# Class-ordered tokens, separate transpose banks and 72-query dilated tiles in a fused attention and MLP kernel

## Chip, core and metric

The kernel runs on one core of one Trainium2 chip. Its engines are TensorE (PE; its weight loads are listed apart as PEld), VectorE (DVE), ScalarE (ACT), GpSimd (POOL) and SyncE (SP, which here only issues transfers). The metric is the device time of that core in microseconds (us), lower is better. Three timed runs of the kernel before gave 463.66, 466.44 and 466.76 us; the median is 466.44 us.

## What is computed

Eight batches, eight heads, 576 tokens, head size 64. Heads 0 to 3 attend to the last 32 tokens; heads 4 to 7 to 32 tokens in steps of 4 (the same residue modulo 4). The result, 4608 tokens by 512, goes through a two-layer MLP with a swish-like gate.

```python
rel = pos[:, None] - pos[None, :]
mask_plain = (rel >= 0) & (rel < 32)
mask_dil = (rel >= 0) & (rel < 32 * 4) & (rel % 4 == 0)
attn = softmax(where(mask, q @ k.T / 8, -1e9))       # heads 0-3 plain, 4-7 dilated
x = (attn @ v).transpose(0, 2, 1, 3).reshape(8 * 576, 512)
h = x @ w_in                                         # 512 -> 2048
out = (h / (1 + exp(-beta * h))) @ w_out             # 2048 -> 512, float32
```

## The kernel before, in words

Every engine executes its instructions in program order, and the order is written out by hand. Attention of one batch is a list of 44 named steps (`STEPS`). The MLP works on nine tiles of 512 tokens (t = 0 to 8); tile t is 16 `slot_h` (four matmuls of 512 columns into a bank of `psum_h`, two banks; then a tanh on ACT and a `g` on DVE) and 16 `slot_o` (four matmuls each; four slots complete one block of 128 tokens in the only bank of `psum_o`, then ACT copies it to `osb` and SP stores it). Attention of batch 0 runs alone; after that the loop over t issues the slots of tile t with the steps of batch t + 1 between them, about one and a half steps a slot. Eight `slot_o` of a tile follow its last `slot_h`, the other eight are mixed into the next tile. Tiles 7 and 8 have no attention beside them, and the last tile ends with 16 `slot_o`.

Heads are handled in pairs x = 0 to 3 (x = 0, 1 plain, called h = 0; x = 2, 3 dilated, h = 1). Steps:

- T (`step_t`, two for each x): a row of the loaded q or k holds four consecutive tokens, T = 0 to 3 being the residue modulo 4. Six transposes of 96 rows (L192) fill one bank `tp` with k and q of two residues. DVE then copies k to `kT` (L201), ACT half of q to `qz` (L202), DVE the other half (L203). For h = 0 the copies write with a step of four elements, because `kT` and `qz` are in token order; for h = 1 they are in class order (residue after residue), and the copies write runs.
- S (`step_s`): two matmuls give the scores of two query tiles of 96 against 128 keys (L210), ACT takes the exponential into `pt` (L216), DVE multiplies by a mask (L220).
- V (`step_v`): four matmuls (L230) into the only bank of `psum_pv`; DVE takes the reciprocal of the sums (L236) and scales (L238) into `xs`.
- X (`step_x`): two transposes (L252) into a `tp` bank, and one to four ACT copies (L271) into `xT`, split where a tile of 512 tokens or a residue ends. For h = 1 these write with a step of four.

The two `tp` banks are shared by T and X. `extras(b)` says beside which step POOL casts the next batch (`cast_qk`, `cast_v`) and SP loads the one after (`load_qk`, `load_v`, `fill_v`). The dilated v is loaded by 12 transfers in rows of 256 bytes. `first` does the same for batch 0 and for the weights, which POOL issues. `tick` issues a store two slots after its block.

Of the kernel before, what the change touches and what calls it, by code (L numbers as in the profile page):

```python
# [23 lines left out]
def kernel(  # L24
# [17 lines left out]
    WIN = 32  # L42
    QT = 96
# [36 lines left out]
    kT = [const_pool.tile([P, WIN + S], BF16, name=f"kT{i}") for i in range(4)]  # L80
    qz = [const_pool.tile([P, 2, S], BF16, name=f"qz{i}") for i in range(4)]
    pt = [const_pool.tile([P, NI * 2 * QT + WIN], BF16, name=f"pt{i}") for i in range(4)]
    vaug = [[const_pool.tile([P, NI, 4, D + 1], BF16, name=f"vaug{p}{h}") for h in range(2)]
            for p in range(2)]
    vst = [vstage_pool.tile([P, NI, 4, D], FP32, name=f"vst{h}") for h in range(2)]
    xT = {}


    def zeros():
        for i in range(4):  # L90
            nc.vector.memset(qz[i][64:128, 0, :], 0.0)
            nc.vector.memset(qz[i][0:64, 1, :], 0.0)
            nc.vector.memset(kT[i][:, 0:WIN], 0.0)
            nc.vector.memset(pt[i][:, NI * 2 * QT:], 0.0)
        for p in range(2):
            for h in range(2):
                nc.vector.memset(vaug[p][h][:, :, :, D:D + 1], 1.0)
        for h in range(2):
            nc.vector.memset(vst[h][0:WIN, :, :, :], 0.0)

    def build_masks():
        pp = masks["PP"]
        flat = pp[:].rearrange("p a b n -> p (a b) n")
        nc.gpsimd.memset(flat, 1.0)

        nc.gpsimd.affine_select(
            out=flat, in_=flat, pattern=[[0, 4], [-1, QT]], base=-1, channel_multiplier=1,
            compare_op=ALU.is_ge, fill=0.0)
        nc.gpsimd.affine_select(
            out=flat, in_=flat, pattern=[[0, 4], [1, QT]], base=WIN, channel_multiplier=-1,  # L110
            compare_op=ALU.is_ge, fill=0.0)
        for name, m in masks.items():
            if name == "PP":
                continue
            nc.vector.tensor_copy(out=m[:], in_=pp[:])
            for a in range(2):
                if name[a] == "F":
                    nc.vector.memset(m[0:WIN, a, :, :], 0.0)
                if name[a] == "M":
                    nc.vector.memset(m[0:80, a, :, 48:QT], 0.0)  # L120

    def build_beta():
        tpb = psum_pv.tile([P, 4, P], FP32, name="pv")
        nc.tensor.transpose(tpb[:, 0, 0:NFB], beta_row[:, :], ident_f[:, :])
        nc.vector.tensor_single_scalar(
            out=beta_half[:], in_=tpb[:, 0, 0:NFB], scalar=0.5, op=ALU.mult)
# [300 lines left out]
```

## Time and profile before

| what | value |
|---|---|
| median of three runs | 466.44 us |
| the profiled execution | 463.03 us, span of its instructions 461.3 us |
| PE busy | 356.1 us (77% of the span), 2305 matmuls and transposes |
| PEld busy | 180.7 us (39%) |
| DVE busy | 263.7 us (57%) |
| ACT busy | 228.8 us (50%) |
| POOL busy | 81.1 us (18%) |
| mean granted TensorE clock | 0.925 of 2.4 GHz |

Busy times are shares of the whole span. The span has stages with different limits: attention of batch 0 alone, seven tiles with attention beside the MLP, two tiles of MLP alone. Matmuls are pipelined, so the time from the start of one to the start of the next says more than the length of one.

### The profile page before, as it was taken

To read this page: it belongs to the slowest core of one execution; us is meant where nothing else is said; L and a number is where in the kernel's file an instruction comes from. 1 tells how busy PE (TensorE), PEld (TensorE's weight loads), DVE (VectorE), ACT (ScalarE), POOL (GpSimd) and SP (SyncE) were. 2 spreads that over 40 slices of the span, in tenths; PEclk is the share of its full clock that TensorE was granted. 3 is DMA by queue.
4 is the path that set the end of the run, shared out by engine and by line. 5 is a ranking of instruction groups with operands and counts; after the bars stand their busy time and mean duration, and the time that the engine had idled before them with its cause. 6 is when DMAs were issued, how large, how long until landed. Compare 5 with 4: busy or idle time off the path is not lost.

```text
span 461.3 us, 6491 instructions
## 1 busy us (share of the span) xinstructions
PE 356.1 (77%) x2305; PEld 180.7 (39%) x2305; DVE 263.7 (57%) x604; ACT 228.8 (50%) x515; POOL 81.1 (18%) x119
## 2 busy tenths in 40 slices
PE   1156577859886978867985798697886899999986
PEld 0133343424443434434442454343443444444432
DVE  7676568456853667267736765466726682532510
ACT  1245366536554456435743565345643665544521
POOL 2243445025000520044003400052000000000000
PEclk9999999977998789959997989878995999999999
DMA  8989987930555015710862055500020001001011
GB/s 204 203 166 214 195 194 186 240 87 1 134 133 147 1 52 133 181 50 1 185 163 68 0 140 129 148 1 31 0 77 0 11 14 60 33 24 45 23 47 69
DMA packets 68609, 43.72 MB, mean 95 GB/s; under 512 B 40912, under 2 KB 63456, under 8 KB 68576
## 3 DMA queue, kind: packets, MB, share of 16 engines
q1 hardware_dynamic: 61920, 37.62, 32.3%
q0 software_dynamic: 4224, 4.19, 5.5%
q10 hardware_dynamic: 2432, 1.48, 1.4%
q8 instruction: 18, 0.29, 0.3%
q14 instruction: 15, 0.12, 0.1%
HBM read 36.71 MB, written 9.44 MB: 100 GB/s over the span
## 4 chain that ended last, share of the span: by engine, by line
PE 38%; DVE 10%; ACT 7%; issue 1%; POOL 0%; ACTq 0%
PE o_ps L302 19%; PE h_ps L286 15%; DVE g L293 3%; ACT tnh L290 3%; DVE kT L201 2%; ACT osb L307 2%; ACT qz L202 2%; DVE qz L203 2%; DVE pt L220 1%; PE pv L230 1%; PE sc L210 1%; DVE xs L238 1%; PE tp L192 1%; PE tp L252 1%; ACT pt L216 0%
## 5 line engine op out<-in xcount | busy, mean ns | idle before, releaser
L286 PE MATMUL h_ps<-xT,w_in_bf 128*128 128x512 bf16 x576 | 159.8, 408 | 0.8 <-DVE g L293 0.7
L293 DVE SCALAR_TENSOR_TENSOR g<-tnh,h_ps 128x512 bf16<-128x512 bf16 x144 | 98.9, 687 | 104.2 <-ACT tnh L290 102.9
L302 PE MATMUL o_ps<-w_out_bf,g 128*128 128x512 bf16 x576 | 149.7, 395 | 9.8 <-ACT osb L307 9.8
L290 ACT ACTIVATE tnh<-h_ps,beta_half 128x512 bf16<-128x512 f32 x144 | 98.6, 685 | 51.5 <-PE h_ps L286 51.5
L176 POOL CAST qkb<-stage 96x512 bf16<-96x512 f32 x84 | 49.5, 627 | 199.4 <-PE tp L192 162.3
L202 ACT COPY qz<-tp 64x288 bf16<-64x288 bf16 x64 | 37.8, 591 | 88.2 <-DVE kT L201 88.2
L302 PEld LDWEIGHTS <-g 128*128 128x128 bf16 x576 | 54.6, 101 | 62.3 <-issue 18.3
L192 PE MATMUL tp<-ident_b,qkb 96*128 96x96 bf16 x384 | 34.0, 242 | 58.2 <-DVE qz L203 38.7
L286 PEld LDWEIGHTS <-w_in_bf 128*128 128x128 bf16 x576 | 55.3, 104 | 50.6 <-issue 11.6
L203 DVE COPY qz<-tp 64x288 bf16<-64x288 bf16 x64 | 35.5, 555 | 42.4 <-ACT qz L202 42.4
L192 PEld LDWEIGHTS <-qkb 96*128 96x128 bf16 x384 | 28.6, 117 | 74.0 <-issue 44.6
L271 ACT COPY xT<-tp 128x96 bf16<-128x96 bf16 (+4 forms) x174 | 42.3, 355 | 18.9 <-PE tp L252 18.9
L230 PE MATMUL pv<-vaug,pt 128*128 128x65 bf16 x384 | 30.1, 203 | 26.6 <-DVE xs L238 25.9
L307 ACT ACTIVATE osb<-o_ps 128x512 f32<-128x512 f32 x36 | 21.5, 597 | 54.9 <-PE o_ps L302 54.9
L216 ACT ACTIVATE pt<-sc 128x384 bf16<-128x384 f32 x96 | 45.5, 482 | 6.1 <-PE sc L210 6.1
L230 PEld LDWEIGHTS <-pt 128*128 128x128 bf16 x384 | 21.7, 103 | 55.1 <-DVE xs L238 44.1
L238 DVE TENSOR_TENSOR xs<-pv,rcp 96x256 bf16<-96x256 f32 x96 | 40.3, 420 | 3.3
L210 PE MATMUL sc<-qz,kT 128*128 128x192 bf16 x192 | 35.2, 274 | 5.4 <-ACT pt L216 5.3
L201 DVE COPY kT<-tp 128x288 bf16<-128x288 bf16 x64 | 35.1, 549 | 1.1 <-PE tp L192 0.3
L210 PEld LDWEIGHTS <-kT 128*128 128x128 bf16 x192 | 19.6, 109 | 27.0 <-issue 15.1
L179 POOL CAST vaug<-vst 128x1536 bf16<-128x1536 f32 x16 | 23.8, 1490 | 33.2 <-DMA vst<-in_v_dram 24.2
L236 DVE RECIPROCAL rcp<-pv 96x4 f32<-96x4 f32 x96 | 16.7, 174 | 21.3 <-PE pv L230 21.2
(40 smaller groups left out, 102.4 us busy)
## 6 DMA issues: line engine op xcount, KB each, us to landing
out_dram<-osb SPq DMA_DIRECT2D x36, 256.0 KB, 2.0
stage<-in_k_dram SPq DMA_DIRECT2D x16, 384.0 KB, 4.7
stage<-in_q_dram SPq DMA_DIRECT2D x14, 384.0 KB, 5.8
vst<-in_v_dram SPq DMA_DIRECT2D x96, 48.0 KB, 3.8
vst<-in_v_dram SPq DMA_DIRECT2D x30, 144.0 KB, 5.9
stage<-in_q_dram SPq DMA_DIRECT2D x16, 192.0 KB, 4.9
stage<-in_k_dram SPq DMA_DIRECT2D x14, 192.0 KB, 4.6
w_in_bf<-in_moe_w_in_dram POOLq DMA_DIRECT2D x4, 512.0 KB, 7.4
```

Source lines behind the costliest of these rows:

```text
L176: (eng.copy if eng is nc.scalar else eng.tensor_copy)(out=o[:, hp], in_=i[:, hp])
L192: nc.tensor.transpose(tp[:, j, c * QT:(c + 1) * QT], src[:, c, hp, 2 * tt + j].rearrange("p a d -> p (a d)"), ident_b[0:QT, 0:QT])
L202: nc.scalar.copy(out=view(qd[0:64, 0, :]), in_=tp[0:64, :, 144:288])
L203: nc.vector.tensor_copy(out=view(qd[64:128, 1, :]), in_=tp[64:128, :, 144:288])
L210: nc.tensor.matmul(sc[:, a, 0:2 * QT], lhsT=kT[x][:, i * QT:i * QT + P], rhs=qz[x][:, :, i * QT:(i + 1) * QT], start=True, stop=True)
L216: nc.scalar.activation(out=w.rearrange("p (a n) -> p a n", a=2), in_=sc[:, :, 0:2 * QT], func=ACT.Exp, scale=SCALE)
L230: nc.tensor.matmul(pv[:, h4, 0:D + 1], lhsT=pt[2 * h + hp][:, c:c + P], rhs=vaug[b % 2][h][:, i, h4, :], start=True, stop=True)
L238: nc.vector.tensor_tensor(out=xs[:], in0=pv[0:QT, :, 0:D], in1=rcp[0:QT, :].unsqueeze(2).to_broadcast([QT, 4, D]), op=ALU.mult)
L286: nc.tensor.matmul(hps[:], lhsT=w_in_bf[:, kt, fb * P:(fb + 1) * P], rhs=xT[t][:, kt, :], start=(kt == 0), stop=(kt == NKT - 1))
L290: nc.scalar.activation(out=tnh[:], in_=hps[:], func=ACT.Tanh, scale=beta_half[:, fb:fb + 1])
L293: nc.vector.scalar_tensor_tensor(out=g[:], in0=tnh[:], scalar=1.0, in1=hps[:], op0=ALU.add, op1=ALU.mult)
L302: nc.tensor.matmul(ops[:], lhsT=g_t[t, fb][:, tb * P:(tb + 1) * P], rhs=w_out_bf[:, fb, :], start=(fb == 0), stop=(fb == NFB - 1))
```

## The change

All tokens stay in class order (residue after residue in each batch) from the load to the output rows. Part by part:

- T is split in K (`step_k`) and Q (`step_q`), four each, with eight transposes in a bank of their own. K has one DVE copy of 576 columns, for x = 0, 1 reading the bank with a step and writing runs. Q has two copies of 576 columns by one engine: DVE for x = 1, else ACT.
- Dilated queries are cut into tiles of 72 (one class is 144): for x = 2, 3 four S steps of 2 x 144 columns and four V steps of two tiles; for x = 0, 1 three S steps and two V steps of three tiles. A V step now works on one pair of heads.
- X: three or four transposes in one bank and one ACT copy of 288 columns, eight a batch. `xT` is one tensor for all 4608 tokens.
- Dilated v comes in two transfers with rows of 1 KB.
- Blocks of 128 rows are stored by class, one transfer for each class that they touch. `osb` has two buffers instead of three, and in the last tile every other block uses a bank of `psum_h`.
- Order: 42 steps; `at_once` lets 3, 2, then 1 block of a tile (4 in the last) follow its last `slot_h`, the rest is mixed into the next tile. Steps are paced by weights (`WORK`), with twice as many beside a `slot_o` as beside a `slot_h`. Loads of dilated v, weights and the next batches are issued beside other steps.

```diff
 STEPS = (
-    "T00 T01 T02 T03 T10 S000 T11 S010 T12 S001 T13 S011 S002 V00 S012 V01 S100 V02 X00 "
-    "S110 V03 X01 S101 V04 X02 S111 V05 X03 S102 V10 X04 S112 V11 X05 V12 X10 V13 X11 V14 "
-    "X12 V15 X13 X14 X15"
+    "K0 Q0 K1 Q1 S00 K2 S01 Q2 S02 K3 S10 Q3 S11 V00 S12 V01 S20 X00 S21 V10 S22 X01 V11 S23 "
+    "X10 S30 V20 X11 S31 V21 S32 V22 X20 S33 V23 V30 X21 V31 V32 X30 V33 X31"
 ).split()
...
-    osb_pool = pool("osb", 3)
+    osb_pool = pool("osb", 2)
...
-    xT = {}
+    xT = const([P, NKT, B * S], BF16, "xT")
...
+        else:
+            rows = v[b, 4:8].rearrange("h (t T) d -> t h (T d)", T=C)
+            e(0).dma_start(out=vd_st[0:96, 0].rearrange("p h T d -> p h (T d)"), in_=rows[0:96])
+            e(1).dma_start(out=vd_st[:, 1].rearrange("p h T d -> p h (T d)"), in_=rows[16:CT])
...
+    def transposes(b, x, chunks, lo):
+        h, hp = divmod(x, 2)
         src = qkb[b, h]
+        tp = psum_tp.tile([P, 1024], BF16, name="tp")
+        tv = tp[:, 0:8 * QT].rearrange("p (T t) -> p T t", T=C)
+        for T in range(C):
+            for i, c in enumerate(chunks):
                 nc.tensor.transpose(
+                    tv[:, T, i * QT:(i + 1) * QT],
+                    src[:, c, hp, T].rearrange("p a d -> p (a d)"), ident_b[0:QT, 0:QT])
+        return tv[:, :, lo:lo + CT]
+
+    def step_k(b, x):
+        tv = transposes(b, x, (0, 1), 0)
+        if x < 2:
+            nc.vector.tensor_copy(
+                out=kT[x][:, WIN:].rearrange("p (t T) -> p t T", T=C),
+                in_=tv.rearrange("p T t -> p t T"))
         else:
+            nc.vector.tensor_copy(out=kT[x][:].rearrange("p (T t) -> p T t", T=C), in_=tv)
+
+    def step_q(b, x):
+        tv = transposes(b, x, (1, 2), 48)
+        copy = nc.vector.tensor_copy if x == 1 else nc.scalar.copy
+        copy(out=qz[x][0:64, 0], in_=tv[0:64])
+        copy(out=qz[x][64:128, 1], in_=tv[64:128])
...
+    def step_v(b, x, j):
+        h, hp = divmod(x, 2)
+        n, m = (QT, 3) if x < 2 else (HT, 2)
+        pv = psum_pv.tile([P, 512], FP32, name="pv")
...
+            nc.scalar.copy(
+                out=o.rearrange("p T (i u) -> p T i u", i=3),
+                in_=xp[:, 0:m * n].rearrange("p (i T u) -> p T i u", i=3, T=C))
         else:
+            nc.scalar.copy(out=o, in_=xp[:, 0:m * n].rearrange("p (T t) -> p T t", T=C))
...
         if part == 0:
-            o_t[t, tb] = psum_o.tile([P, HD], FP32, name="o_ps")
+            if t == NTT - 1 and tb % 2:
+                o_t[t, tb] = psum_h.tile([P, HD], FP32, name="h_ps")
+            else:
+                o_t[t, tb] = psum_o.tile([P, HD], FP32, name="o_ps")
...
+               lambda: load_w_in(1), lambda: load_w_in(2), lambda: load_w_in(3),
+               lambda: load_qk(1, 0, [SQ]), lambda: load_v(1, 0, [SQ])],
+        "S00": [build_beta],
+        "S20": [lambda: load_w_out(0), lambda: load_w_out(1)],
+        "S22": [lambda: load_w_out(2), lambda: load_w_out(3),
+                lambda: load_qk(1, 1, [SQ]), lambda: load_v(1, 1, [SQ])],
...
+    at_once = [3, 2] + [1] * (NTT - 3) + [4]
+    WORK = {"K": 3, "Q": 4, "S": 3, "V": 3, "X": 2}
...
+        room = [(1 if fn is slot_h else 2) for fn, *_ in slots[:-2]]
+        total, whole, done, seen = sum(room), sum(WORK[s[0]] for s in STEPS), 0, 0
```

For t = 3 to 6 this gives the order (h and o are slots): h K0 h Q0 o K1 Q1 h o S00 K2 h S01 o Q2 S02 h K3 h S10 o Q3 h S11 o V00 S12 h V01 o S20 X00 h S21 h V10 o S22 X01 h V11 o S23 X10 h S30 o V20 X11 h S31 h V21 o S32 V22 h X20 o S33 V23 h V30 o X21 V31 o V32 X30 o V33 X31 o o. The tiles have 28, 28, 28, 32, 32, 32, 32, 32 and 44 slots, before 24, then 32 seven times, then 40.

## Rows read from the trace of the kernel before

**Rows 1.** Stretches: PE, PEld, DVE, ACT, POOL busy us (count); PE clock, DMA share, GB/s.

```profile
9.50:45.50 36.00, 16.41 (x145) 10.90 (x146) 25.47 (x64) 15.82 (x41) 12.73 (x16) 1.00 1.05 194
45.50:92.50 47.00, 34.84 (x243) 17.94 (x242) 29.56 (x68) 25.49 (x65) 16.97 (x22) 1.00 0.91 204
...
241.40:291.60 50.20, 40.75 (x274) 20.85 (x273) 29.68 (x68) 26.48 (x58) 9.81 (x14) 0.90 0.38 95
...
390.10:419.40 29.30, 27.93 (x130) 12.50 (x129) 11.01 (x16) 13.38 (x20) 0.00 (x0) 1.00 0.10 36
419.40:461.30 41.90, 35.31 (x161) 15.50 (x159) 10.99 (x16) 15.17 (x23) 0.00 (x0) 0.99 0.12 44
```

**Rows 2.** Timeline, last tile, one of four blocks: start us, us, engine line, operation [idle before].

```profile
445.24 3.61 PE L302 MATMUL o_ps<-w_out_bf,g 128*128 128x512 bf16 x16 [0.69 <-ACT osb L307]
```

**Rows 3.** Timeline of tile 4's T steps.

```profile
242.27 0.68 PE L192 MATMUL tp<-ident_b,qkb 96*128 96x96 bf16 x12
...
243.79 0.79 DVE L201 COPY kT<-tp 128x288 bf16<-128x288 bf16 x1
...
244.62 0.79 ACT L202 COPY qz<-tp 64x288 bf16<-64x288 bf16 x1 [1.46 <-DVE kT L201]
245.44 0.80 DVE L203 COPY qz<-tp 64x288 bf16<-64x288 bf16 x1 [0.85 <-ACT qz L202]
...
246.28 0.42 PE L192 MATMUL tp<-ident_b,qkb 96*128 96x96 bf16 x6 [2.48 <-DVE qz L203]
...
256.56 0.30 DVE L201 COPY kT<-tp 128x288 bf16<-128x288 bf16 x1
...
256.90 0.39 ACT L202 COPY qz<-tp 64x288 bf16<-64x288 bf16 x1 [0.87 <-DVE kT L201]
```

**Rows 4.** Stretches of tile 4; columns as in rows 1.

```profile
241.40:257.40 16.00, 10.71 (x73) 5.80 (x72) 9.47 (x16) 6.72 (x12) 4.81 (x7) 0.79 0.18 54
257.40:268.50 11.10, 8.66 (x55) 4.36 (x53) 8.01 (x20) 6.02 (x14) 5.00 (x7) 0.87 0.00 0
268.50:280.60 12.10, 12.10 (x88) 6.00 (x85) 8.47 (x22) 8.72 (x19) 0.00 (x0) 0.98 0.74 176
280.60:291.60 11.00, 9.28 (x66) 4.69 (x66) 3.73 (x12) 5.02 (x15) 0.00 (x0) 1.00 0.68 160
```

**Rows 5.** Waits over the span: who waited for whom, us, times, longest us.

```profile
ACT qz L202 <- DVE kT L201: 88.2, 64, 4.7
...
DVE qz L203 <- ACT qz L202: 42.4, 64, 0.9
...
PE pv L230 <- DVE xs L238: 25.9, 27, 2.7
...
ACT pt L216 <- PE sc L210: 6.1, 15, 1.2
```

**Rows 6.** Groups by line and shape, tile 4: count, busy us, mean ns, idle before.

```profile
L293 DVE SCALAR_TENSOR_TENSOR g<-tnh,h_ps 128x512 bf16<-128x512 bf16 x16 | 11.0, 686 | 11.5 <-ACT tnh L290 11.3
L290 ACT ACTIVATE tnh<-h_ps,beta_half 128x512 bf16<-128x512 f32 x16 | 10.9, 684 | 5.2 <-PE h_ps L286 5.2
...
L216 ACT ACTIVATE pt<-sc 128x384 bf16<-128x384 f32 x12 | 5.7, 481 | 0.7 <-PE sc L210 0.7
L238 DVE TENSOR_TENSOR xs<-pv,rcp 96x256 bf16<-96x256 f32 x12 | 5.0, 420 | 0.4
...
L236 DVE RECIPROCAL rcp<-pv 96x4 f32<-96x4 f32 x12 | 2.1, 173 | 3.2 <-PE pv L230 3.2
```

**Rows 7.** Timeline of batch 0: the cast on DVE, first and last of twelve V.

```profile
21.29 3.37 DVE L176 CAST qkb<-stage 96x512 bf16<-96x512 f32 x6
...
29.30 0.42 PE L230 MATMUL pv<-vaug,pt 128*128 128x65 bf16 x4
...
44.15 0.40 PE L230 MATMUL pv<-vaug,pt 128*128 128x65 bf16 x4 [0.57 <-DVE xs L238]
```

**Rows 8.** Transfers in the first 92.5 us, by queue of issue: KB each, us to landing.

```profile
w_out_bf<-in_moe_w_out_dram POOLq DMA_DIRECT2D x4, 512.0 KB, 13.9
```

More of the change, by code (lines that the diff above doesn't have):

```diff
@@ L80 @@
[L80 to L85, printed above, removed]
-    xT = {}
-    def zeros():
[L90 to L99, printed above, removed]
+    const = lambda shape, dt, name: const_pool.tile(shape, dt, name=name)
@@ new lines, in zeros @@
+    def zeros():
+        nc.vector.memset(warm[:], 0.0)
+        nc.scalar.activation(out=warm[:], in_=warm[:], func=ACT.Exp)
+        for x in range(4):
+            nc.vector.memset(qz[x][64:128, 0], 0.0)
+            nc.vector.memset(qz[x][0:64, 1], 0.0)
+            nc.vector.memset(pt[x][:, pt_w[x]:], 0.0)
+            if x < 2:
+                nc.vector.memset(kT[x][:, 0:WIN], 0.0)
+        for i in range(2):
+            nc.vector.memset(vp[i][:, :, :, D:D + 1], 1.0)
+            nc.vector.memset(vd[i][:, :, :, :, D:D + 1], 1.0)
+        nc.vector.memset(vp_st[0:WIN], 0.0)
+        nc.vector.memset(vd_st[96:128, 0], 0.0)
@@ L109, in build_masks @@
         nc.gpsimd.affine_select(
[L110 to L120, printed above, removed]
+            out=flat, in_=flat, pattern=[[0, 4], [1, C], [C, QT // C]], base=WIN,
@@ L122, in build_beta @@
     def build_beta():
[L123 to L124 removed]
+        tpb = psum_pv.tile([P, 512], FP32, name="pv")
+        nc.tensor.transpose(tpb[:, 0:NFB], beta_row[:, :], ident_f[:, :])
         nc.vector.tensor_single_scalar(
[L126 removed]
+            out=beta_half[:], in_=tpb[:, 0:NFB], scalar=0.5, op=ALU.mult)
     def load_w_in(g):
@@ L366 @@
     for n, name in enumerate(STEPS):
-        for fn in first.get(n, []) + e.get(n, []):
+        for fn in first.get(name, []) + e.get(n, []):
             fn()
         attention_step(0, name)
+    at_once = [3, 2] + [1] * (NTT - 3) + [4]
+    WORK = {"K": 3, "Q": 4, "S": 3, "V": 3, "X": 2}
+    left = []
     for t in range(NTT):
         slots = []
+        n = len(left)
         for fb in range(NFB):
             slots.append((slot_h, t, fb))
-            if t and fb % 2:
-                slots.append((slot_o, t - 1, 2 + fb // 8, (fb // 2) % 4))
-        for tb in range(2):
-            slots += [(slot_o, t, tb, part) for part in range(4)]
-        if t == NTT - 1:
-            for tb in (2, 3):
-                slots += [(slot_o, t, tb, part) for part in range(4)]
+            while left and n - len(left) < n * (fb + 1) // NFB:
+                slots.append(left.pop(0))
+        left = [(slot_o, t, tb, part) for tb in range(4) for part in range(4)]
+        slots += left[:4 * at_once[t]]
+        left = left[4 * at_once[t]:]
         b = t + 1
@@ L385 @@
         e = extras(b) if b < B else {}
-        total, last = len(work), len(slots) - 3
+        room = [(1 if fn is slot_h else 2) for fn, *_ in slots[:-2]]
+        total, whole, done, seen = sum(room), sum(WORK[s[0]] for s in STEPS), 0, 0
         for n, (fn, *args) in enumerate(slots):
             fn(*args)
-            while work and (total - len(work)) * last < total * (n + 1):
+            seen += room[n] if n < len(room) else 0
+            while work and done * total < whole * seen:
                 m, name = work.pop(0)
+                done += WORK[name[0]]
                 for x in e.get(m, []):
```

267 lines of the change are left out of this document (130 added, 137 removed).

## The prediction

> **What bounds the kernel now.** I cut the span into stretches first, at the first `slot_h` of each tile [rows 1]. Attention of batch 0 runs until 45.5 us, tile 0 takes 47.0, tiles 1 to 6 run from 92.5 to 390.1 (49.6 each), tile 7, without attention, 29.3, and tile 8 41.9. The reader is to compare tile 4 with tile 7: both have 32 slots, yet one takes 50.2 and the other 29.3. Neither DVE (29.7 busy) nor ACT (26.5) comes near 50 us.
>
> What would tile 4 cost if PE never waited? Tile 7 has two places where a block follows a block and must wait 0.69 for the only bank [rows 2], so a slot takes (29.3 - 1.4) / 32 = 0.87 us and 32 take 27.9. Six more transposes lengthen a row from 0.42 to 0.68 us [rows 3], 0.043 each; 48 make 2.1. In the stretch from 268.5 to 280.6 PE is never idle [rows 4]; its 88 rows are 12 slots (10.5 us) and five each of S, V and X in the other 1.6, so all twelve cost 3.9. Together 33.9: about 16 us of the 50.2 are lost.
>
> The four stretches of tile 4 show where [rows 4]. The first 16.0 us have six slots and seven of the eight T steps, some 7.3 us of work, at a granted clock of 0.79: nearly 9 lost. The next 11.1 lose about 4.6, then nothing, then about 2. The whole list of waits names the cause of the first [rows 5]: ACT's `qz` copies wait 88.2 us for DVE's `kT`, DVE's `qz` 42.4 for ACT, and PE's transposes then wait for DVE. The timeline shows it [rows 3]: three copies of one bank stand one behind the other, 0.79 to 0.80 us each in token order, and PE's next transposes wait 2.48 us behind them. In class order the same copies take 0.30 and 0.39. The waits of V for `xs` (25.9) come from the only `pv` bank.
>
> **The change, part by part.** *K and Q.* One engine reads each bank now, so the chain DVE, ACT, DVE goes. PE: 64 transposes for 48, 2.8 us a batch (+0.7). DVE: a copy has about 0.17 fixed, what four columns take in L236 [rows 6]; 288 columns in runs add 0.13 [rows 3], so 576 cost 0.43. That holds for K2, K3 and both halves of Q1. K0 and K1 read the bank with a step, which no row shows. Bounds: 0.43 if the step is free, and 0.17 + 576 x 2.15 ns = 1.41 if it costs what the stepped writes cost now ((0.79 - 0.17) / 288 = 2.15 ns). I take one column at a time as in L238 ((0.42 - 0.17) / 256 = 0.98 ns): 0.73, since runs are written and only the read is stepped. DVE a batch: 29.7, less 8.7 for T (eight copies of 0.79, eight of 0.30), plus 2 x 0.73 + 4 x 0.43 = 3.2, plus 0.5 for wider `xs`: 24.7, or 26.1 at the upper bound.
>
> The Trainium skill bears on this, page "VectorE: DVE Perf Modes", section "What auto-detection actually checks": a 16-bit copy takes two elements a cycle only where every operand has unit step. That speaks against K0 and K1 and would give them about 0.77 (estimate). By the same rule the stepped write of today would cost about 0.47, but the trace has 0.79 to 0.80 for it [rows 3], so a step can cost more than the rule says.
>
> ACT: from 0.39 for 288 columns and 0.48 for 384 [rows 3, 6] I take about 0.85 ns a further column. A Q copy of 576 columns is then 0.63, six of them 3.8 instead of 4 x 0.79 + 4 x 0.39 = 4.7. Exponentials: six of 0.48 and eight of 0.40, 6.1 for 5.7. X: one copy of 0.39 instead of up to four short ones. ACT stays at or below 26 us.
>
> *S, V, X.* 28 score matmuls for 24 (the same columns), 56 of V for 48, 28 transposes for 24: at most one sixth more of 3.9, so 4.5. PE without waits in tiles 3 to 6: 27.9 + 2.8 + 4.5 = 35.2; in tiles 1 and 2, with 28 slots, 31.7.
>
> *Waits that remain.* PE, ACT and DVE work in order, so I walk through the new order of tiles 3 to 6. At the head, Q1 needs the bank that ACT reads for Q0, behind two tanh of 0.68: about 0.5. A V that follows a `slot_h` has its `rcp` and `xs` on DVE behind that slot's `g`, which waits for the tanh: 0.68 + 0.69 + 0.6 = 2.0 after the slot's end [rows 6]. The next V needs the same bank; where only a `slot_o` and an S (1.0) lie between, as before V22, PE waits about 1.1. So V01 waits 0.8, V11 0.3, V22 1.1, V30 0.3, V31 0.5, and X31 0.8 for V33's `xs`. Eviction of the block at the end of a tile costs 0.69 once instead of twice, but falls beside V30. I sum 4.3: 39.5 a tile, from 35.2 (all hidden) to 43.5 (lost as in 257.4 to 291.6 now, nearly 7, and the head). Tiles 1 and 2: 31.7 + 4.8 = 36.5. Tile 0: 31.7, three blocks at its end (+2 x 0.69), its V chain (5) and first waits for late loads (1.5): 39.5.
>
> *Start.* The T chain of batch 0 goes; casts and loads keep their pace. PE begins at about 9.5 as now; K0 to Q1 and S00 end near 15, DVE then casts the second half (3.4, rows from 21.29), K2 to Q3 end near 22, and twelve V follow each other at the pace of now, (44.15 - 29.30) / 11 = 1.35 [rows 7], until near 37; with X31 38 for 45.5.
>
> *Loads and POOL.* The dilated v goes from 12 issues to 2, and 64 rather than 36 stores are issued on SP; neither queue's time is on the path while SP idles. Stores stand behind loads issued at X31; with two `osb` buffers and 3.5 us between blocks this is covered, and costs ACT the delay if a load blocks SP for longer. POOL issues `w_out` behind the casts of batch 1, near 30 us; now it lands 13.9 after issue [rows 8], and the first `slot_o` comes near 58. DMA is nearly full until then [rows 1], so up to 10 us could show; I put 1.5 in tile 0.
>
> *End.* Tile 7: 27.9 + 0.69 = 28.6. Tile 8 has 44 slots: 38.4, one wait of 0.69 (four now, since other blocks use another bank), and the same end as now, 41.9 - 34.9 - 2.8 = 4.2: 43.3.
>
> *Sum.* 38 + 39.5 + 2 x 36.5 + 4 x 39.5 + 28.6 + 43.3 = 380.4 of span; with the 1.7 us around it 382.1, against 463.03 for the profiled execution. The median shown stands 3.4 above that execution, so I forecast 385.
>
> **Rivals.**
> - *In-order coupling or late loads.* Waits reach 43.5 a tile in tiles 1 to 6, or `w_out` holds tile 0 for 10 us and K0, K1 cost 1.41: 385 + 6 x 4 = 409, or 385 + 10 + 8 = 403; both, 425. For it: 4.6 of 11.1 us are lost now in a stretch with no T chain to speak of [rows 4]. Against: the next stretch loses nothing at one and a half steps a slot.
> - *Nearly all waits hidden.* 37 a tile: 385 - 6 x 2.5 = 370, with a quick start 365. Against: one `pv` bank.
> - *Transposes paced one by one.* If the 16 transposes more a batch could not overlap, at the 0.2 us that one alone lasts (0.42 less five times 0.043), they would cost 3.2 a batch, 26 in all: 411. Against: twelve in 0.68 us [rows 3]. The Trainium skill, page "TensorE: Matmul & The Clock Gate", part 4 (PE-mode transpose), gives about 275 ns in a kernel; by it the sum would be about 420 (estimate).
> - *The head does not shorten.* Q's copies on ACT hold PE as the chain does now: only start, tail and about 4 us a tile are gained, 425 to 440.
> - *Slower: one `xT` for all tiles.* If waits go by tensor, every X copy waits for the last `slot_h` and the next `slot_h` for the copy: 0.87 + 0.39 behind a tanh of 0.68, about 1.9, eight a batch: 15 a tile, 106 in seven, 491. It decides from 11.6 us a tile. Against: `pt` is one tensor of many steps too, and the list of waits shows ACT's writes to it waiting only for scores [rows 5], not for V, which reads other columns.
>
> **How the numbers follow.** Forecast 0.73 (its own range 370 to 404); coupling or late loads 0.15 (404 to 425); nearly hidden 0.05; head 0.02; one by one 0.01; the tensor-wise waits 0.04, three quarters of it above 471. That leaves faster by over 1% at 0.95, within 1% 0.02, slower 0.03; 1% is about what a measurement of this kernel can tell from no change. The range 369 to 408 leaves out some 0.2: most of the slow half of the coupling cases, the fast end, and the rivals above it.
>
> **What would show it.** Right: no wait of ACT `qz` for DVE `kT`; a first third of tile 4 with no PE gap over 1 us; tiles 3 to 6 at 38 to 41; granted clock near 1.0; the largest PE wait is V for `xs`. K0, K1 on DVE near 0.73. Wrong: tiles above 43 with PE waiting on `g` or `pt`; the first `slot_o` waiting for `w_out`; waits between `xT` copies and `slot_h` of another tile; stepped reads above 1.4.

## The result and the profile after

The changed kernel takes 403.38 us (median of four runs, 400.9 to 405.25) where the kernel before takes 465.05 beside it: a ratio of 0.868, 95% interval 0.860 to 0.875. The forecast was 385. The profiled execution took 402.49 us with a span of 400.6, so nearly all of the miss lies inside the span: 400.6 against a sum of 380.4. Each kernel's time below is the median of four runs, and one of the four of "token order" (429.2 us, over 1.5% above the fastest) is a slow one, without which its median is 421.8 instead of 423.1.

The first view to read is the same as for the kernel before, the span cut at the first `slot_h` of each tile; the columns are those of [rows 1].

```profile
0.00:45.20 45.20, 16.97 (x177) 12.60 (x178) 27.17 (x80) 13.25 (x29) 21.93 (x38) 0.85 1.10 227
45.20:86.50 41.30, 35.72 (x291) 19.68 (x292) 27.19 (x60) 23.95 (x47) 13.71 (x17) 0.96 1.01 217
86.50:126.60 40.10, 33.66 (x289) 18.64 (x288) 27.22 (x60) 24.29 (x47) 10.38 (x14) 1.00 0.52 118
126.60:166.60 40.00, 34.39 (x290) 19.08 (x289) 27.26 (x60) 23.81 (x47) 10.43 (x14) 0.96 0.54 126
166.60:207.20 40.60, 36.33 (x305) 19.84 (x304) 27.29 (x60) 24.61 (x48) 10.43 (x14) 1.00 0.47 114
207.20:247.90 40.70, 36.43 (x305) 19.88 (x304) 27.29 (x60) 24.60 (x48) 10.43 (x14) 1.00 0.54 124
247.90:288.60 40.70, 36.44 (x305) 19.86 (x304) 27.29 (x60) 24.60 (x48) 10.43 (x14) 1.00 0.27 67
288.60:328.60 40.00, 36.44 (x306) 19.89 (x305) 24.65 (x60) 24.60 (x48) 0.00 (x0) 1.00 0.10 28
328.60:357.10 28.50, 27.81 (x130) 12.57 (x129) 11.00 (x16) 13.38 (x20) 0.00 (x0) 1.00 0.11 38
357.10:400.56 43.46, 38.26 (x177) 17.02 (x175) 10.99 (x16) 15.78 (x24) 0.00 (x0) 1.00 0.17 49
```

Each line stands against one term of the forecast's sum:

| stretch | forecast, us | measured, us | miss |
|---|---|---|---|
| start | 38 | 45.2 (before 45.5) | +7.2 |
| tile 0 | 39.5 | 41.3 | +1.8 |
| tiles 1, 2 | 36.5 each | 40.1, 40.0 | +7.1 |
| tiles 3 to 5 | 39.5 each | 40.6, 40.7, 40.7 | +3.5 |
| tile 6 | 39.5 | 40.0 | +0.5 |
| tile 7 | 28.6 | 28.5 | -0.1 |
| tile 8 | 43.3 | 43.5 | +0.2 |

The misses add up to 20.2 us. Seven tenths of it stand in two places: the start, which did not shrink at all, and tiles 1 and 2, whose 28 slots cost as much as 32 (1.6 us of tile 2 are a dip of the granted clock in this execution, shown further down). Tile 6 is the line to remember: it is the only tile beside attention without POOL work, and it has 2.6 us less of DVE work and takes 0.6 to 0.7 us less than its neighbours.

The second view is the timeline at the head of tile 4, which answers [rows 3].

```profile
208.10 0.51 PE L201 MATMUL tp<-ident_b,qkb 96*128 96x96 bf16 x8
...
209.63 0.75 DVE L209 COPY kT<-tp 128x576 bf16<-128x576 bf16 x1
...
210.10 0.62 ACT L218 COPY qz<-tp 64x576 bf16<-64x576 bf16 x1
...
210.73 0.63 ACT L219 COPY qz<-tp 64x576 bf16<-64x576 bf16 x1
...
211.41 0.50 PE L201 MATMUL tp<-ident_b,qkb 96*128 96x96 bf16 x8 [0.39 <-ACT qz L219]
...
211.95 0.45 DVE L218 COPY qz<-tp 64x576 bf16<-64x576 bf16 x1
...
215.02 0.44 DVE L213 COPY kT<-tp 128x576 bf16<-128x576 bf16 x1
```

DVE and ACT now copy at the same time from two banks, and the head's only PE wait is 0.39 where the kernel before had 2.48. The whole list of waits, columns as in [rows 5], shows what is left; no wait of `qz` for `kT` is among its long ones.

```profile
DVE g L302 <- ACT tnh L299: 96.2, 102, 5.3
...
PE pv L255 <- DVE xs L262: 28.7, 38, 2.2
...
PE tp L201 <- DVE qkb L179: 12.0, 5, 8.4
```

### The profile page after: what moved, and what is told of

It is laid out like the page before. It is cut to its first block, busy times and chain, and to the rows that moved or that the text cites. A ratio compares the mean times of both kernels' runs of the same rounds, so it can differ in the third digit from the quotient of the medians.

```text
span 400.6 us, 6727 instructions
## 1 busy us (share of the span) xinstructions
PE 332.5 (83%) x2561; PEld 179.0 (45%) x2561; DVE 237.3 (59%) x532; ACT 212.9 (53%) x406; POOL 87.7 (22%) x125
## 4 chain that ended last, share of the span: by engine, by line
PE 58%; DVE 17%; ACT 15%; issue 5%; DMA 4%; ACTq 0%
PE o_ps L325 23%; PE h_ps L294 23%; ACT tnh L299 5%; DVE g L302 5%; DVE xs L262 5%; PE pv L255 4%; DVE pt L240 4%; ACT pt L239 3%; PE tp L201 3%; ACT qz L219 2%; ACT qz L218 2%; DMA beta_row<-in_moe_beta_dram 2%; DMA vp_st<-in_v_dram 2%; PE tp L271 2%; PE sc L237 2%
## 5 line engine op out<-in xcount | busy, mean ns | idle before, releaser
L325 PE MATMUL o_ps<-w_out_bf,g 128*128 128x512 bf16 x544 | 137.5, 380 | 1.7 <-ACT osb L330 1.7
L239 ACT ACTIVATE pt<-sc 128x288 bf16<-128x288 f32 (+1 forms) x112 | 49.1, 444 | 33.5 <-PE sc L237 32.5
L255 PEld LDWEIGHTS <-pt 128*128 128x128 bf16 x448 | 23.6, 101 | 52.1 <-DVE xs L262 44.0
L262 DVE TENSOR_TENSOR xs<-pv,rcp 72x256 bf16<-72x256 f32 (+1 forms) x96 | 44.6, 465 | 3.3
L237 PE MATMUL sc<-qz,kT 128*128 128x144 bf16 (+1 forms) x224 | 36.2, 245 | 0.0
L255 PE MATMUL pv<-vd,pt 128*128 128x65 bf16 x256 | 19.4, 200 | 18.2 <-DVE xs L262 18.2
L240 DVE TENSOR_TENSOR pt<-pt,mask_PP 128x384 bf16<-128x384 bf16 x32 | 23.1, 721 | 10.2 <-ACT pt L239 10.2
L281 ACT COPY xT<-tp 128x288 bf16<-128x288 bf16 x32 | 12.7, 397 | 30.4 <-PE tp L271 30.4
L240 DVE TENSOR_TENSOR pt<-pt,mask_d 128x288 bf16<-128x288 bf16 x64 | 21.5, 336 | 7.8 <-ACT pt L239 7.0
L271 PE MATMUL tp<-ident_b,xs 72*128 72x72 bf16 (+1 forms) x224 | 21.3, 208 | 5.2 <-DVE xs L262 5.2
L258 DVE RECIPROCAL rcp<-pv 72x4 f32<-72x4 f32 (+1 forms) x96 | 17.1, 178 | 13.9 <-PE pv L255 13.8
L255 PE MATMUL pv<-vp,pt 128*128 128x65 bf16 x192 | 12.0, 200 | 10.6 <-DVE xs L262 10.5
```

Of the source, the lines that this page charges most:

```text
L237: nc.tensor.matmul(sc[:, a, 0:2 * n], lhsT=lhsT, rhs=rhs, start=True, stop=True)
L239: nc.scalar.activation(out=w, in_=sc[:, :, 0:2 * n], func=ACT.Exp, scale=SCALE)
L240: nc.vector.tensor_tensor(out=w, in0=w, in1=mask, op=ALU.mult)
L255: nc.tensor.matmul(pv[:, a, h2, :], lhsT=pt[x][:, c:c + P], rhs=rhs, start=True, stop=True)
L262: nc.vector.tensor_tensor(out=xs_t[b, x, jx][:, a0:a0 + m], in0=pv[0:n, :, :, 0:D], in1=rcp[0:n, 0:m].unsqueeze(3).to_broadcast([n, m, 2, ...
L271: nc.tensor.transpose(xp[:, a * n:(a + 1) * n], xs[:, a].rearrange("p h d -> p (h d)"), ident_b[0:n, 0:n])
```

## The experiments

Lengths in the table run from the first tanh of a tile to the first of the next, because some traces miss a few matmul records while all 144 tanh are there in each; the last column is the median of the timed runs.

| kernel | first tanh at | tile 0 | 1 | 2 | 3 to 5, each | 6 | 7 | 8 | median, us |
|---|---|---|---|---|---|---|---|---|---|
| before | 47.4 | 46.1 | 49.5 | 50.4 | 49.1 to 50.6 | 47.9 | 29.3 | 40.9 | 465 |
| after | 47.2 | 40.4 | 40.1 | 40.0 | 40.7 | 40.0 | 28.5 | 42.4 | 403.4 |
| banks alone | 42.9 | 48.3 | 45.5 | 46.3 | 45.7 to 46.4 | 45.6 | 29.3 | 40.9 | 438.8 |
| token order | 46.8 | 45.1 | 43.3 | 41.5 | 42.7 to 44.0 | 41.6 | 28.5 | 42.4 | 423.1 |
| v in 256 bytes | 50.4 | 41.7 | 40.1 | 38.4 | 40.7 | 40.0 | 28.5 | 42.5 | 406.2 |
| beta later | 40.1 | 41.3 | 41.5 | 38.4 | 40.7 | 40.0 | 28.5 | 42.4 | 398.0 |
| two pv banks | 46.3 | 39.5 | 39.6 | 35.8 | 38.4 | 37.9 | 28.5 | 42.4 | 387.4 |
| both | 39.4 | 41.8 | 41.1 | 35.8 | 38.4 | 37.9 | 28.5 | 42.4 | 383.4 |
| no cast | 47.1 | 40.9 | 38.8 | 37.1 | 40.0 | 40.0 | 28.5 | 42.4 | 397.3 |
| two at once | 47.4 | 38.1 | 39.7 | 39.7 | 39.7 | 39.5 | 29.3 | 39.0 | 395.4 |
| all three | 38.0 | 35.4 | 39.8 | 38.8 | 38.8 | 38.8 | 29.3 | 39.0 | 377.8 |
| casts moved | 37.8 | 49.3 | 38.8 | 38.8 | 38.8 | 38.8 | 29.3 | 39.0 | 390.5 |

### Which part brought the gain

**Banks alone.** The kernel before with only the separate banks for k and q; tokens in their old order.

```diff
-        tp = psum_tp.tile([P, 2, 512], BF16, name="tp")
+        kp = psum_tp.tile([P, 2, 512], BF16, name="tp")
+        qp = psum_tp.tile([P, 2, 512], BF16, name="tp")
...
-        nc.vector.tensor_copy(out=view(qd[64:128, 1, :]), in_=tp[64:128, :, 144:288])
+        nc.scalar.copy(out=view(qd[64:128, 1, :]), in_=qp[64:128, :, 48:192])
```

> The kernel before with one part of the change alone: each T step puts k and q in banks of their own (eight transposes instead of six), DVE copies k, ACT both halves of q; order of steps, token order, tiles and loads are those of before. Theory: the chain DVE, ACT, DVE on one bank is what cost the first 16 us of a tile; without it the copies of ACT (four T steps of 1.6 and four of 0.8 us, with the tanh between) limit that stretch to about 12 to 13 us: 435 to 446 us. Rival: banks alone suffice and the stretch shrinks to 8 us: 405 to 415. Other rival: ACT becomes the chain with its stepped copies and nothing is gained: 460 to 468.

Measured: 438.8 us, ratio 0.945 (0.942 to 0.947). Its list of waits:

```profile
PE tp L194 <- ACT qz L205: 34.2, 28, 1.9
...
PE pv L232 <- DVE xs L240: 22.2, 28, 1.4
```

The chain from DVE to ACT and back is gone, but ACT now has both stepped copies of a bank, and PE waits 34.2 us for them. The banks alone give 26 of the 62 us.

**Token order.** The changed kernel with q of the plain heads put back in token order, and with it the plain masks and the plain X copies, which then read their bank with a step. All the rest stays; k of the plain heads is in token order in the changed kernel too.

```diff
-        copy(out=qz[x][0:64, 0], in_=tv[0:64])
-        copy(out=qz[x][64:128, 1], in_=tv[64:128])
+        order = ((lambda a: a.rearrange("p T t -> p (T t)").rearrange("p (t T) -> p T t", T=C))
+                 if x < 2 else (lambda a: a))
+        copy(out=order(qz[x][0:64, 0]), in_=tv[0:64])
+        copy(out=order(qz[x][64:128, 1]), in_=tv[64:128])
```

> In the changed kernel the plain queries go back to token order: Q0 and Q1 write with a step of four, the plain masks are in token order, and the plain X copies read their bank with a step; banks, steps, order and loads stay. Theory: once each bank has one reader, stepped copies cost their engine time only, about 1.4 us for each of four copies instead of 0.63 and 0.45, and a longer wait of Q1 for Q0's bank at the head of a tile: 1.5 to 2.5 us a tile, 414 to 422 us. Rival: class order is what made the change fast, half of the gain of 62 us goes: 430 or more.

Measured: 423.1 us, ratio 0.910 (0.906 to 0.915), 18 to 20 us above the changed kernel, at the upper end of the theory's range or one above it. The timeline of its tile 4 (ACT's two copies, then DVE's):

```profile
221.27 1.42 ACT L220 COPY qz<-tp 64x576 bf16<-64x576 bf16 x1
...
222.70 1.43 ACT L221 COPY qz<-tp 64x576 bf16<-64x576 bf16 x1
...
224.18 0.50 PE L201 MATMUL tp<-ident_b,qkb 96*128 96x96 bf16 x8 [1.99 <-ACT qz L221]
...
224.72 1.44 DVE L220 COPY qz<-tp 64x576 bf16<-64x576 bf16 x1 [1.73 <-PE tp L201]
```

Writing in steps costs 1.42 to 1.46 us where writing runs cost 0.45 on DVE and 0.62 on ACT, and the wait at the head goes from 0.39 to 1.99. ACT's X copies of 288 columns take 0.40 with the stepped read as without it. So class order of the plain queries is worth 18 to 20 us in the changed kernel. Banks alone leave stepped copies; class order alone should leave the chain, but that half was not run. Nor were the tiles of 72 queries, the single X copies or the paced order of steps taken out by themselves, so what is left of the 62 us is not shared out among them.

**Rows of 256 bytes.** Dilated v in eight transfers with short rows, where the change has two.

```diff
-            e(0).dma_start(out=vd_st[0:96, 0].rearrange("p h T d -> p h (T d)"), in_=rows[0:96])
-            e(1).dma_start(out=vd_st[:, 1].rearrange("p h T d -> p h (T d)"), in_=rows[16:CT])
+            for T in range(C):
+                e(0).dma_start(out=vd_st[0:96, 0, :, T, :], in_=rows[0:96, :, T, :])
+                e(1).dma_start(out=vd_st[:, 1, :, T, :], in_=rows[16:CT, :, T, :])
```

> The changed kernel, but the dilated v comes in eight transfers with rows of 256 bytes instead of two with rows of 1 KB. Theory: the row size hides behind other work from tile 1 on, and even in the start the cast of v by POOL waits for it off the path: 401 to 407 us, tiles 3 to 6 unchanged at 40.0 to 40.7. Rival (the transfers, full until about 86 us, hold the start or tile 0): start plus tile 0 grow by more than 5 us from their 86.5, 408 us or more.

Measured: 406.2 us, ratio 0.874 (0.869 to 0.878), within the theory's range and with an interval that overlaps that of the changed kernel (0.860 to 0.875). In the profiled run the first tanh comes at 50.4 for 47.2 and tile 0 takes 1.3 more; tiles 3 to 8 are the same within 0.1. The trace has the 1 KB rows matter only at the start and in tile 0; the difference of the medians, 2.8 us, is not clear of the noise.

### Why the start did not shrink

The changed kernel at its start:

```profile
14.02 0.80 PE L201 MATMUL tp<-ident_b,qkb 96*128 96x96 bf16 x8 [2.45 <-ACT qz L219]
...
19.69 0.25 PE L134 MATMUL pv<-ident_f,beta_row 16*128 16x16 f32 x1 [4.87 <-DMA beta_row<-in_moe_beta_dram]
...
19.87 0.50 PE L237 MATMUL sc<-qz,kT 128*128 128x192 bf16 x2
...
21.21 3.99 DVE L179 CAST qkb<-stage 96x512 bf16<-96x512 f32 x6
...
27.94 0.51 PE L255 MATMUL pv<-vp,pt 128*128 128x65 bf16 x6
```

Q1's transposes are done at 14.8. The next matmul on PE is the transpose of `beta_row`, which lands at 19.7, and the first scores stand behind it in program order. The DVE cast of the second half follows the copies and the first mask, at 21.21: the same time as before, 21.29 [rows 7]. The theory was that this one small transpose holds the start.

```diff
-        "S00": [build_beta],
+        "S10": [build_beta],
```

> The transpose of beta, which the changed kernel issues before S00, is issued before S10 instead; nothing else moves. Theory: PE works in order and in the start of the changed kernel waits 4.9 us for the transfer of beta before S00, and DVE's cast of the second half then follows 5 us later than planned; without that wait the first slot of tile 0 comes at 40 to 41 us instead of 45.2, and the whole takes 398 to 399 us. Rival: the second half of q and k (or the dilated v) has not landed earlier than about 19 us, so the cast waits for DMA instead and the time stays at 402 to 404.

Measured: 398.0 us, ratio 0.856 (0.851 to 0.861). Its start:

```profile
14.54 0.52 PE L237 MATMUL sc<-qz,kT 128*128 128x192 bf16 x2
...
16.01 2.09 DVE L179 CAST qkb<-stage 96x512 bf16<-96x512 f32 x6
...
20.02 0.25 PE L134 MATMUL pv<-ident_f,beta_row 16*128 16x16 f32 x1 [0.20 <-DMA beta_row<-in_moe_beta_dram]
```

The row lands at the same time, but PE now reaches its transpose with 0.20 of waiting left. The cast begins 5.2 us earlier and is also shorter, 2.09 for 3.99: here POOL is idle beside it, while in the changed kernel POOL issues the loads of `w_in` and casts beside it, and one of the six pieces takes 1.83 instead of 0.41. The first `slot_h` comes 6.6 earlier, at 38.6: the 38 of the forecast. So the 6.6 us are the wait for beta and, behind it, the longer cast. Of the 6.6 us, 5.4 reach the median; in the profiled run tile 0 and tile 1 give back 1.0 and 1.4, the latter at a granted clock of 0.96 instead of 1.00.

The granted clock of the start was 0.85 in the profiled run of the changed kernel; a cut into 2 us shows 0.50 (1.2 GHz) from about 32 to 48 us, after PE had been busy 0.62 and 0.74 us of two stretches of 2 us. It is no cause of the miss: the kernels "two at once" and "no cast" have the same start at a clock of 1.00 throughout, and their first tanh comes at 47.4 and 47.1.

### Why a tile is not 39.5, and why 28 slots cost 40

**Two pv banks.** One bank of `psum_sc` becomes the second of `psum_pv`.

```diff
-    psum_sc = psum("psum_sc", 2)
-    psum_pv = psum("psum_pv", 1)
+    psum_sc = psum("psum_sc", 1)
+    psum_pv = psum("psum_pv", 2)
```

> One bank is taken from the scores and given to the V steps: two banks for pv, one for sc. Theory: the waits of V for xs, which come from the only pv bank, are the largest wait left (about 4 us of each tile of 40.7, and they pace the V steps of the start); they go, and the waits of S for the exponential that come instead are smaller because slots stand between S steps: tiles at 37 to 38.5 and 385 to 392 us in all. Rival: the exponential stands on ACT behind a tanh and the q copies, so S waits as much as V did: 400 to 408 us.

Measured: 387.4 us, ratio 0.834 (0.831 to 0.836), 16 us less than the changed kernel. The waits of PE for `xs` at L255, 28.7 us before, are gone from the list; these come in their place:

```profile
PE tp L271 <- DVE xs L262: 10.2, 18, 0.9
...
PE sc L237 <- ACT pt L239: 5.1, 11, 1.1
```

Each tile from 3 to 6 loses 2.1 to 2.3 us, tile 2, with 28 slots, 4.2, and of this 1.6 are not the bank's: in the profiled run of the changed kernel the clock dipped there. A cut of that tile into 2 us shows it (columns as above); its length is 38.4 in "beta later" and "v in 256 bytes", which have the same tile at a full clock. Tile 1 loses only 0.5 and stays at 39.6, because something else holds it. PE's largest wait in tile 1 of the changed kernel, and in tile 2:

```profile
PE h_ps L294 <- DVE g L302: 3.7, 4, 2.2
```

```profile
PE pv L255 <- DVE xs L262: 4.9, 4, 2.1
```

Tile 1 waits for `g`, and 3.5 of these 3.7 us are still there with two banks; tile 2 waits for `xs`. The clock in tile 2, in the changed kernel:

```profile
140.00:142.00 2.00, 1.04 (x7) 0.31 (x4) 2.00 (x2) 1.79 (x4) 2.00 (x4) 1.00 0.00 0
142.00:144.00 2.00, 0.85 (x11) 0.62 (x12) 1.97 (x6) 0.34 (x1) 1.55 (x1) 1.00 0.50 142
144.00:146.00 2.00, 2.00 (x11) 1.00 (x9) 1.56 (x5) 1.37 (x4) 0.00 (x0) 0.59 0.65 169
```

PE was idle for about half of 4 us, waiting for a V's `xs`, while DVE was busy without a break; then the clock fell. The same 4.9 us of waiting, with the same longest of 2.1, left the clock at 1.00 in "beta later" and "v in 256 bytes". So a wait can be followed by a loss beyond its length, and was in one of these three runs.

**No cast.** What kept DVE busy there is a mask. Beside POOL's casts a mask multiply of the changed kernel takes up to 2.0 us, against 0.35 elsewhere:

```profile
102.10 1.95 DVE L240 TENSOR_TENSOR pt<-pt,mask_PP 128x384 bf16<-128x384 bf16 x1 [1.52 <-ACT pt L239]
...
102.67 1.17 POOL L179 CAST qkb<-stage 96x512 bf16<-96x512 f32 x2
...
103.97 0.68 DVE L302 SCALAR_TENSOR_TENSOR g<-tnh,h_ps 128x512 bf16<-128x512 bf16 x1
...
104.70 1.02 PE L294 MATMUL h_ps<-xT,w_in_bf 128*128 128x512 bf16 x4 [2.22 <-DVE g L302]
```

This is tile 1. The `g` behind the mask is late, its `psum_h` bank comes free late, and PE waits 2.22 us with a `slot_h` that has nothing to do with attention. The groups of DVE, first of tile 4, then of tile 6, where POOL does nothing:

```profile
L302 DVE SCALAR_TENSOR_TENSOR g<-tnh,h_ps 128x512 bf16<-128x512 bf16 x16 | 11.0, 686 | 9.8 <-ACT tnh L299 9.7
L240 DVE TENSOR_TENSOR pt<-pt,mask_PP 128x384 bf16<-128x384 bf16 x4 | 3.6, 892 | 1.1 <-ACT pt L239 1.1
```

```profile
L240 DVE TENSOR_TENSOR pt<-pt,mask_PP 128x384 bf16<-128x384 bf16 x4 | 1.4, 351 | 1.5 <-ACT pt L239 1.5
```

The mean falls from 892 to 351 ns. `g` has 686 beside the casts, as it had before [rows 6]. The Trainium skill, page "SBUF — State Buffer", section "Who interferes with whom", says that a DVE instruction with two inputs in SBUF contends with GpSimd instructions that read SBUF, and one with at most one such input, outside the two-port modes, does not. The trace agrees: the mask reads `pt` and a mask, both in SBUF, while `g` reads one of its tensors from PSUM.

The test leaves out the casts.

```diff
-            at("S10", lambda: cast_qk(b + 1, 0, 0, G))
+            if b == 0: at("S10", lambda: cast_qk(b + 1, 0, 0, G))
...
-        src = qkb[b, h]
+        src = qkb[min(b, 1), h]
```

> The changed kernel without GpSimd's casts for batches 2 to 7: their attention works on the cast q and k of batch 1 and the cast v of batches 0 and 1; all loads, matmuls and copies stay. Theory: GpSimd's casts slow DVE's mask multiplies beside them (721 ns in the mean for the plain mask), and that holds the tiles: the mask falls to about 0.35 us, the tiles 0 to 5 lose 0.7 us each (as tile 6, which has no casts, shows), those with 28 slots up to 3: 393 to 400 us. Rival (DVE is off the path, and tile 6 is shorter by chance): 401 to 404 us.

Measured: 397.3 us, ratio 0.855 (0.851 to 0.859). The mask's mean over the span:

```profile
L240 DVE TENSOR_TENSOR pt<-pt,mask_PP 128x384 bf16<-128x384 bf16 x32 | 11.6, 364 | 12.6 <-ACT pt L239 12.6
```

364 ns for 721. Tiles 3 to 5 come to 40.0, the length of tile 6, and tiles 1 and 2 to 38.8 and 37.1; of tile 2's 2.9 us some 1.6 are again the clock. In tile 4 the wait that shrinks is that of V01, behind the mask of 1.05 us; the changed kernel's row is

```profile
224.60 0.36 PE L255 MATMUL pv<-vp,pt 128*128 128x65 bf16 x6 [1.50 <-DVE xs L262]
```

and without casts it waits 0.80, the whole 0.7 of the tile. In tile 1 the wait for `g` goes from 3.7 to 2.1. The theory held for tiles 1 to 5: the casts cost 0.7 us in a tile of 32 slots and 1.3 in those of 28. Tile 0 did not fall (40.9 for 40.4).

**Two at once.** Two blocks at the end of every tile, as before the change.

```diff
-    at_once = [3, 2] + [1] * (NTT - 3) + [4]
+    at_once = [2] * (NTT - 1) + [4]
```

> The changed kernel with two blocks at the end of every tile but the last, as before the change: tile 0 has 24 slots instead of 28, tiles 1 and 2 have 32 instead of 28. Theory (a tile beside attention costs about 40 us by its chain of steps through the one pv bank, however few its slots): tile 0 stays within 1.5 us of 41.3, tiles 1 and 2 come out at 40 to 41, 402 to 406 us. Rival (tile 0 to 2 are set by their slots at 0.87 us each): tile 0 falls by 3.5 us to 38, tiles 1 and 2 rise by 3.5 each, 406 to 409 us.

Measured: 395.4 us, ratio 0.850 (0.846 to 0.855), 8 us less than the changed kernel. Both expectations were too high, the theory's by over 6 us: both left out tile 8 (3.4 us) and the 1.0 us of each of tiles 3 to 5. The number of slots is 288 in either kernel. The change takes four each from tiles 1 and 2 and gives four each to tiles 0 and 8. Tile 8 is bound by PE and pays 3.4 us for its four (42.4 for 39.0, and four times 0.87 is 3.5), tile 0 pays 2.3, and tiles 1 and 2 get little back. They are not set by their slots: with 32 they take 39.7 each, with 28 they took 40.1 and, at a full clock, 38.4, so four slots fewer are worth nothing in tile 1 and 1.3 us in tile 2. In tile 1 of the changed kernel only four `slot_o`, left over from tile 0, are mixed with its 16 `slot_h`; with eight, as here, no wait of PE for `g` is in its list of long waits. So the theory has the lengths of tiles 1 and 2 right, but the one pv bank is not what holds tile 1, and it is wrong for tile 0. Tiles 3 to 5 have 32 slots in either kernel and lose 1.0 each: eight slots, not twelve, are mixed into the next tile, so the V steps stand beside others, and in tile 4 their waits for `xs` go from 3.2 to 1.2 us.

### Together

**Both** has the edits of "beta later" and "two pv banks".

> The changed kernel with both repairs: beta's transpose moved from beside S00 to beside S10, and two pv banks with one sc bank. Theory (the two losses lie in different stretches, start and tiles): the gains add, 387.4 - 5.4 = 382, range 380 to 384 us, first slot at 38 to 39, tiles 3 to 6 at 38 to 38.5. Rival (the earlier start runs into loads that are still under way, and gives part of it back in tile 0 or 1): 385 to 388 us.

Measured: 383.4 us, ratio 0.825 (0.821 to 0.829): within the theory's range, with 20 us less than the changed kernel where the two edits alone gave 5.4 and 16.0. The gains nearly add; the first tanh comes at 39.4, tiles 3 to 5 take 38.4.

**All three** adds "two at once".

> The changed kernel with three edits: beta's transpose beside S10, two pv banks with one sc bank, and two blocks at the end of every tile but the last. Theory (blocks moved into the last tile cost 0.87 us a slot there, and tiles 1 and 2, held by their chain, hand nothing back for them): tile 8 falls from 42.4 to 39, tile 0 by 2 to 3, tiles 1 and 2 rise by 0 to 2.6 since two pv banks have freed them, 377 to 381 us against 383.4 with the first two edits. Rival (with two pv banks every tile is set by its slots, so that it does not matter where they stand): 382 to 385 us.

Measured: 377.8 us, ratio 0.813 (0.811 to 0.815): the fastest, 25.6 us below the changed kernel. Tile 0 falls by 6.4 (more than expected), tile 8 by 3.4, tile 1 by 1.3 (its granted clock is 1.00 here, 0.96 in "both"); tile 2 rises by 3.0 (0 to 2.6 expected), tiles 3 to 6 by 0.4 to 0.9, tile 7 by 0.8. All of PE's rows with a wait in its tile 4, 38.8 us:

```profile
194.00 0.50 PE L201 MATMUL tp<-ident_b,qkb 96*128 96x96 bf16 x8 [0.39 <-ACT qz L219]
...
201.66 0.32 PE L237 MATMUL sc<-qz,kT 128*128 128x192 bf16 x2 [0.45 <-ACT pt L239]
...
206.36 0.33 PE L237 MATMUL sc<-qz,kT 128*128 128x192 bf16 x2 [0.23 <-ACT pt L239]
...
218.81 1.02 PE L325 MATMUL o_ps<-w_out_bf,g 128*128 128x512 bf16 x4 [0.44 <-ACT osb L330]
...
223.87 1.02 PE L325 MATMUL o_ps<-w_out_bf,g 128*128 128x512 bf16 x4 [0.43 <-ACT osb L330]
...
226.86 0.24 PE L271 MATMUL tp<-ident_b,xs 72*128 72x72 bf16 x2 [0.66 <-DVE xs L262]
```

They sum to 2.6 us; the rest, 36.2, is PE at work, one above the 35.2 of the forecast's floor (an idle time begins only when the last matmul has drained, so some of the one is waiting too).

**Casts moved** adds to that another place for POOL's casts of q and k. With them the loads of q and k and the cast of the dilated v move too, the latter now ahead of the casts of q and k of h = 1.

```diff
-            at("S10", lambda: cast_qk(b + 1, 0, 0, G))
+            at("S32", lambda: cast_qk(b + 1, 0, 0, G))
...
+            at("K0", lambda: cast_qk(b, 1, 0, G))
```

> The same three edits, and GpSimd's casts of q and k moved away from the plain masks: those of h = 0 from beside S10, S11, S12 to beside S32, S33, V23 of the step list before, those of h = 1 from beside S30, S31, S32 to beside K0, Q0, K1 of their own batch. Theory (GpSimd's casts slow DVE's masks, and that costs mainly in the first tiles): the plain mask falls to about 0.4 us from 0.74 to 0.87, the tiles 0 and 1 lose 1 to 3 us each, later ones up to 0.7: 2 to 6 us below the kernel without this edit. Rival (the casts now slow the kT copies at the head and the dilated masks instead, or come late for the next K0): no gain, or up to 3 us slower, with PE waiting for GpSimd's qkb.

Measured: 390.5 us, ratio 0.841 (0.838 to 0.843): 12.7 us slower than "all three", worse than either expectation. Tile 1 gains 1.0 us and tiles 2 to 6 nothing, all 38.8: with two pv banks the slow masks have room. Tile 0 loses 14:

```profile
51.19 1.89 POOL L185 CAST vd<-vd_st 128x2048 bf16<-128x2048 f32 x1 [11.25 <-DMA vd_st<-in_v_dram]
53.02 3.40 POOL L179 CAST qkb<-stage 96x512 bf16<-96x512 f32 x6
```

PE's transposes of K2 at 53.69 wait 8.37 us for that cast, which stands on POOL behind a cast of v that waits for its load until 51.19, while the transfers are full; behind that wait the granted clock is 0.50 from 54 to 60 us. The rival named the right cause, the casts that come late for batch 1, and sized it too low. What moving them is worth without that was not tried; tiles 1 to 6 together gain about 1 us.

## Why the prediction was right and where it failed

- *The chain of copies* went as forecast. No `qz` copy waits long for a `kT` copy, no PE gap in the head of tile 4 is over 0.39 us, and the granted clock is 1.00 in tiles 1 and 3 to 8. K0 and K1 cost 0.75 (0.73 forecast, 0.43 to 1.41 bounded), K2, K3 and Q1 0.44 to 0.46 (0.43), Q on ACT 0.62 to 0.63 (0.63), the X copy 0.40 (0.39). The 0.63 is partly luck: the two rows that it is drawn from (0.39 for 288 columns, 0.48 for 384) give 0.94 ns a column, not 0.85, and 0.66.
- *The upper bound of 1.41* was the price of a stepped write, 2.15 ns a column; "token order" measured 1.42 to 1.46 for that. The step is cheap where it is read and dear where it is written, as the forecast chose.
- *Floor and waits of tiles 3 to 6.* 39.5 forecast, 40.0 to 40.7 measured. The walk named the right waits; most were right in size: counted from start to start, V22 waits 1.11 (1.1 forecast), X31 0.81 (0.8), Q1 0.56 (0.5). V01 was sized at 0.8 and measured 1.67, because a mask ahead of its `xs` takes 1.05 beside a cast. All seven make 5.4 where 4.3 was forecast, and 35.2 and 5.4 are the 40.6 measured.
- *DVE at 24.7 a batch* is the term behind it that was mis-sized: 27.3 with casts, 24.65 in tile 6. The sum took the masks as they stand in the trace of before without asking what POOL does beside them.
- *Tiles 1 and 2 at 36.5* failed in tile 1. The walk of a 32-slot tile was carried over, with 0.5 us more of waits and four slots fewer. Tile 2 comes near that: of its 3.5 us above the forecast 1.6 are the clock and 1.3 the casts ("no cast" has it at 37.1); in that run its waits of V for `xs` are 3.6 us, against 2.5 in tile 3 with 32 slots, so with less cover the waits grow, by more than the 0.5. Tile 1 is at 38.8 without casts. It waits for something that the walk did not have, `g`: 3.7 us, and 2.1 without casts. The likely reason, not tested alone, is its order, in which `slot_h` follow each other with few `slot_o` between. "Two pv banks" leaves it at 39.6, and "two at once" shows that the four slots were worth nothing here, and 1.3 us in tile 2.
- *Start at 38.* The step "K0 to Q1 and S00 end near 15" failed. The diff hangs `build_beta` ahead of S00, and the walk did not count that transpose or ask when its input lands: the rule that every instruction of a moved step counts, broken for one row of 16 partitions. With that removed the start is 38.6. The cast behind it took 3.99 us for 3.4, and V's pace was 1.46 us start to start for 1.35; without the wait they are 2.09 and 1.33.
- *Tile 0* took 1.8 more. No wait for `w_out` is in the list of long waits; what the 1.8 us are was not taken apart. Tiles 7 and 8 came within 0.2.
- *The rivals.* The total, 403.4, lies at the lower end of the in-order and late-load rival (403 to 425; its own terms, 24 and 18 us, add up to 427) and at the upper end of the likeliest case's own range (370 to 404). That the stated range of 369 to 408 holds it is owed to the width of the range more than to the sum: beta's transpose stands in no sentence of the forecast, and the waits of tiles 1 and 2 only in a rival that has them at another size. Neither told the mechanism whole: tiles did not reach 43.5 and `w_out` did not hold tile 0, but the loss is of that rival's kind, PE waiting in order behind a late transfer and behind a late `g`. No tensor-wise wait on `xT` shows, and eight transposes take 0.51 us, so they overlap.

## What to carry to other kernels

Before a moved step is costed at nothing, ask of each operand when it lands: one transpose of a late 8 KB row held an in-order engine for 4.9 us, and moving it was worth 5.4 in the median. Work taken from a stretch that is bound by a chain and put where the engine is full costs its whole length and returns little (here 1.3 us for the 5.7 that tiles 0 and 8 paid), so move it the other way. When one engine's turnaround through a single PSUM bank shows in the list of waits, try a second bank first, if another tile can spare one; here it was worth 16 us, more than any other repair.

## What the runs showed of the hardware

A mask multiply of 128x384 took 0.35 us alone and up to 1.95 to 2.00 beside GpSimd's casts, with `g` and `xs` unchanged beside them (686 and 420 ns). DVE's cast of q and k from SBUF to SBUF, one input, took 0.41 us a piece beside an idle POOL and up to 1.83 beside POOL's casts. A bf16 copy of 576 columns out of PSUM took 0.75 us on DVE with a stepped read, 1.43 to 1.46 with a stepped write, 0.45 with neither, and on ACT 1.42 with a stepped write and 0.62 without. ACT's copy of 288 columns took 0.40 with a stepped read or without.
